# Adding two shifted exp readings by an accumulating DMA before PV, in an attention and MLP kernel

## Chip, cores and metric

One core of one Trainium2 chip. The metric is the device time of one launch in microseconds, the median of several runs of the same program. The engines are TensorE (PE in the profile; PEld is its loading of weights), VectorE (DVE), ScalarE (ACT), GpSimd (POOL) and SyncE (SP, which issues most DMAs here).

## The reference

Layer norm of x, then two branches that are added to x: attention with 32 query heads of 20 columns that share one head of keys and values, and an MLP with SiLU. S is 2048, D is 640, F is 1728.

```python
xn = _layernorm(x, axis=-1)
return x + _A_ref(xn, A_wq, A_wk, A_wv, A_wo) + _B_ref(xn, B_w1, B_w2)

# _A_ref, Dh = 20, H = 32
q = (x @ wq).reshape(B, S, H, Dh).transpose(0, 2, 1, 3)
k = x @ wk
v = x @ wv
scores = jnp.einsum("bhqd,bkd->bhqk", q, k) * (Dh ** -0.5)
p = _softmax(scores, axis=-1)
o = jnp.einsum("bhqk,bkd->bhqd", p, v)
o.transpose(0, 2, 1, 3).reshape(B, S, H * Dh) @ wo

# _B_ref
h = _silu(jnp.einsum("bsd,df->bsf", x, w1))
out = jnp.einsum("bsf,fd->bsd", h, w2)
```

## The kernel before

The scores are worked on in blocks of 128 keys by 512 queries of one head. 32 heads, 4 chunks of 512 queries and 16 blocks of keys make 2048 blocks. Four heads of one chunk form a group (64 blocks), and there are 32 groups. Heads sit in four slots of 32 rows or columns, so that TensorE runs up to four small matmuls side by side.

One step, `do_S`, takes three or four blocks. TensorE multiplies keys with queries (S, L1127) into one PSUM bank for each block. There are eight banks of 512 columns, one of which gathers the group's output. Then the blocks of the step are shared out:

- Most go to ScalarE: exp (L1161) over one, two or three banks at once, into a ring of `NBLK` blocks of results, E.
- Up to two go to VectorE: one instruction (L1176) scales and shifts the score so that its 16-bit integer, read as bf16, is a rough exp. Results go to Z, three blocks to a set (`ZB`). When a set is full, `flush_z` has GpSimd add a constant to Z twice (L1202, an integer add over four 16-bit numbers at a time), into Y0 and Y1. These are two more readings of the same rough exp, shifted by a part of an octave. The mean over the three readings, each with its weight, is close to the exp.

The weights are not multiplied onto the readings. V stands in memory three times, each copy scaled by the weight of its reading (`PH`), with a column for the sum of the softmax.

PV (`do_pv`, L968) multiplies these readings with V and adds into the group's bank: one matmul of 32 by 512 for a block from ScalarE, three for a block from VectorE (one each for Z, Y0, Y1). One to four of these, in different slots, run side by side as one set. When a group is done, its bank is copied out (L1245), transposed by a DMA, divided by the sum (L1231, L1236) and kept for the output projection.

Everything else of TensorE (query projections and MLP's first layer at L870 with 512 columns, MLP's second layer and output projection at L870 with 320) is cut into jobs that fill the room between S and PV.

The order of each engine's instructions is fixed when the program is built. A planner (`Sched`, with `step` as TensorE's choice) plays the program through with costs and latencies, and writes out each engine's list as it comes. The rules that choose between S, PV and jobs have some thirty numbers, and `SEG` holds a row of them for each 32 blocks. At run time each engine works its list in order, and waits on semaphores where an operand comes from elsewhere.

At the end no S is left: the last group's PV, the copy (L1245), its transposes on TensorE (L1252), reciprocal and multiply (L1231, L1236), transposes again (L1368), their copy (L1373), and the output projections of the last chunk (L870, 320 columns) follow, with the last evacuations (L1421 on ScalarE, L1424 on VectorE) and stores (L1428).

Of the kernel before, what the change touches and what calls it, by code (L numbers as in the profile page):

```python
# [8 lines left out]
BF16 = mybir.dt.bfloat16  # L9
# [7 lines left out]
P = 128  # L17
# [28 lines left out]
PH = ((0, 1.0), (43, 0.8046875), (86, 0.625))  # L46
ZMAX = 32512.0
# [3 lines left out]
NBLK = 35  # L51
NZ = 8
NY = 4
# [66 lines left out]
            "ACT4", "SPLIT", "U2", "LOOK", "W4", "M3")  # L120
SEG = (
# [366 lines left out]
class Builder:  # L488
# [20 lines left out]
    def alloc(self):  # L509
# [6 lines left out]
        self.qd = sb([P, 2, QW], BF16)  # L516
        self.wo = sb([P, DC, D], BF16)
        self.kT = sb([P, S], BF16)
        self.v = sb([P, 3, KT, SLOT], BF16)
        self.qT = sb([P, QS, QW], BF16)  # L520
        self.E = sb([P, NBLK * QW], BF16)
        self.Z = sb([P, NZ, ZB * QW], U16)
# [55 lines left out]
    def steps_init(self):  # L578
# [12 lines left out]
        self.pe_mode = None  # L591
        self.blk_pos = 0
        self.zset = 0
        self.yset = 0
        self.zblocks = []
        self.exp_op = {}
        self.dve_steps = 0
# [1285 lines left out]
```

## Time and profile before

| | |
|---|---|
| median of 3 runs | 669.32 us (669.15 to 669.32) |
| the profiled execution | 669.12 us, its span 667.3 us |
| granted TensorE clock | 1.00 |
| exp blocks on ScalarE, on VectorE | 1316, 732 |
| matmuls of PV (L968) | 3512 |
| instructions in all | 22800 |

The span runs from the first to the last instruction. The groups of the profile give busy time and the mean duration of one instruction. Durations contain the way through the engine's pipeline, so that consecutive instructions overlap, and the distance between two starts is shorter than a duration. For matmuls the ends are modelled. Idle time of an engine is put down to what ended it.

### The profile page before, as it was taken

How to read it: one execution, taken by the hardware profiler on the slowest of the kernel's cores; microseconds unless marked ns; L12 is line 12 of the kernel's file. 1: busy time of each engine (PE TensorE's matmuls, PEld its weight loads, DVE VectorE, ACT ScalarE, POOL GpSimd, SP SyncE). 2: the span in 40 equal slices, each digit the busy share in tenths (PEclk: the TensorE clock that was granted, in tenths of full speed). 3: DMA queues.
4: the chain of work that ended last, by engine and by line, in shares of the span. 5: the costliest groups of instructions: out<-in, count | busy, mean ns of one | idle time of the engine just before them, and what ended most of it. 6: DMA issues, size and time to landing. Idle time of an engine off the chain costs nothing.

```text
span 667.3 us, 22800 instructions
## 1 busy us (share of the span) xinstructions
PE 659.4 (99%) x9735; PEld 220.4 (33%) x9735; DVE 601.3 (90%) x1085; ACT 647.7 (97%) x737; POOL 404.6 (61%) x509
## 2 busy tenths in 40 slices
PE   8999999999999999999999999999999999999998
PEld 4432233332323322233333323233233333223345
DVE  7888999999989999999889999988999999998783
ACT  7999999999999999999999999999999999999993
POOL 2056457777486656676556653866767674676550
PEclk9999999999999999999999999999999999999999
DMA  7565201010012210000003110000002121001001
GB/s 211 110 213 150 73 14 12 2 26 2 18 44 62 57 10 17 3 10 18 19 10 84 41 32 17 10 10 18 10 13 47 38 57 37 10 10 31 5 11 41
DMA packets 51433, 26.73 MB, mean 40 GB/s; under 512 B 38566, under 2 KB 50694, under 8 KB 51334
## 3 DMA queue, kind: packets, MB, share of 16 engines
q1 hardware_dynamic: 51190, 25.12, 14.5%
q8 instruction: 78, 1.28, 0.8%
q14 instruction: 21, 0.17, 0.1%
q10 hardware_dynamic: 144, 0.16, 0.1%
HBM read 11.44 MB, written 2.62 MB: 21 GB/s over the span
## 4 chain that ended last, share of the span: by engine, by line
PE 87%; ACT 7%; DVE 3%; SPq 1%; DMA 1%; issue 0%; ACTq 0%
PE psall L968 33%; PE psall L1127 28%; PE psall L870 26%; ACT sbt L1161 6%; DVE sbt L1176 2%; ACT sbt L1336 1%; SPq L1531 1%; DMA sbt<-in_A_x_dram 1%; DVE sbt L1424 0%; PE psall L1326 0%; DVE sbt L1236 0%; ACT sbt L1620 0%; DVE sbt L1666 0%; DVE sbt L1771 0%; ACT sbt L1655 0%
## 5 line engine op out<-in xcount | busy, mean ns | idle before, releaser
L1161 ACT ACTIVATE sbt<-psall 128x1024 bf16<-128x1024 f32 (+2 forms) x649 | 620.1, 1129 | 3.5 <-PE psall L1127 2.6
L1202 POOL INT64_ADD sbt<-sbt x492 | 399.7, 827 | 244.4 <-DVE sbt L1176 171.3
L1176 DVE TENSOR_SCALAR sbt<-psall 128x512 uint16<-128x512 f32 x732 | 473.1, 683 | 46.3 <-PE psall L1127 37.1
L968 PE MATMUL psall<-sbt 128*32 128x512 bf16 x3512 | 265.0, 383 | 0.2
L1127 PE MATMUL psall<-sbt 32*128 32x512 bf16 x2048 | 245.8, 384 | 2.1 <-ACT sbt L1161 0.7
L870 PE MATMUL psall<-sbt 128*32 128x320 bf16 (+2 forms) x3923 | 220.7, 331 | 0.5 <-DVE sbt L1176 0.4
L1127 PEld LDWEIGHTS psall<-sbt 32*128 32x128 bf16 x2048 | 61.9, 91 | 241.4 <-ACT sbt L1161 161.1
L870 PEld LDWEIGHTS psall<-sbt 128*32 128x32 bf16 x3923 | 84.6, 95 | 84.6 <-issue 54.4
L968 PEld LDWEIGHTS psall<-sbt 128*32 128x32 bf16 x3512 | 64.4, 95 | 101.3 <-issue 64.6
L1336 ACT ACTIVATE sbt<-psall 128x512 bf16<-128x512 f32 x54 | 39.6, 739 | 0.0
L1341 DVE SCALAR_TENSOR_TENSOR sbt<-sbt,psall 128x512 bf16<-128x512 bf16 x54 | 36.6, 682 | 2.6 <-ACT sbt L1336 1.2
L1245 DVE CAST sbt<-psall 128x512 bf16<-128x512 f32 x32 | 21.8, 681 | 5.4 <-PE psall L968 5.3
L1236 DVE TENSOR_TENSOR sbt<-sbt 128x320 bf16<-128x320 bf16 x31 | 18.3, 591 | 0.1
L846 PE MATMUL psall<-sbt 128*128 128x512 bf16 (+4 forms) x55 | 15.2, 428 | 1.2 <-DVE sbt L1590 1.2
L1424 DVE SCALAR_TENSOR_TENSOR sbt<-psall,sbt 128x320 bf16<-128x320 f32 x28 | 13.1, 477 | 2.9 <-PE psall L870 2.9
L1405 DVE SCALAR_TENSOR_TENSOR sbt<-psall,sbt 128x320 bf16<-128x320 f32 x28 | 13.5, 483 | 1.6 <-PE psall L870 1.4
L1294 DVE TENSOR_SCALAR sbt<-psall 128x512 bf16<-128x512 f32 (+1 forms) x19 | 12.9, 680 | 0.1
L1635 DVE BATCH_NORM_STATS2 sbt<-sbt 128x6 f32<-128x320 bf16 x22 | 10.0, 470 | 0.9 <-DMA sbt<-in_A_x_dram 0.7
L1421 ACT ACTIVATE sbt<-psall 128x320 bf16<-128x320 f32 x4 | 1.7, 438 | 8.7 <-PE psall L870 8.7
L846 PEld LDWEIGHTS psall<-sbt 128*128 128x128 bf16 x55 | 5.5, 109 | 9.1 <-issue 4.0
L1231 DVE RECIPROCAL sbt<-sbt 128x16 f32<-128x16 bf16 x31 | 7.5, 243 | 0.0
L1620 ACT ACTIVATE sbt<-sbt 128x640 bf16<-128x640 bf16 x5 | 3.6, 730 | 3.2 <-DMA sbt<-in_A_x_dram 3.2
(57 smaller groups left out, 70.1 us busy)
## 6 DMA issues: line engine op xcount, KB each, us to landing
sbt<-in_A_x_dram SPq DMA_DIRECT2D x32, 160.0 KB, 3.2
out_dram<-sbt SPq DMA_DIRECT2D x15, 160.0 KB, 2.0
sbt<-in_B_w_dram SPq DMA_DIRECT2D x5, 432.0 KB, 5.3
sbt<-sbt SPq DMA_DIRECT2D x105, 20.0 KB
sbt<-in_B_w_dram SPq DMA_DIRECT2D x13, 160.0 KB, 3.1
sbt<-sbt SPq DMA_TRANSPOSE x58, 2.5
sbt<-in_A_wo_dram SPq DMA_DIRECT2D x5, 160.0 KB, 3.1
sbt<-in_A_wq_dram SPq DMA_DIRECT2D x5, 140.0 KB, 3.1
```

The lines of the kernel that those rows point to most:

```text
L846: return pe.matmul(self.bk(b, 0, n), self.zero[:, 0:P], self.zero[:, 0:n], start=True, stop=True)
L870: ins = pe.matmul(self.bk(b, 0, n, r, r + SLOT), w[:, r:r + SLOT], x, start=start, stop=stop, tile_position=(0, r), skip_group_check=True)
L968: ins = pe.matmul(self.bk(ub[k], 0, QW, r, r + SLOT), self.v[:, it.w, it.kt, :], it.x(), start=f, stop=False, tile_position=(0, r), skip_g ...
L1127: ins = pe.matmul(self.bk(bank[x]), self.kT[r:r + SLOT, kt * P:(kt + 1) * P], self.qT[r:r + SLOT, g % QS, :], start=True, stop=True, tile_ ...
L1161: return a.activation(self.E[:, b0 * QW:(b0 + na) * QW].rearrange("p (b n) -> p b n", n=QW), src, AF.Exp, scale=ACT_SCALE)
L1176: return v.tensor_scalar(self.Z[:, zs, zp * QW:(zp + 1) * QW], self.bk(bb), OFF, ZMAX, ALU.add, ALU.min)
L1202: sc.new("pool", YP_FIX + YP_BLK * n, lambda g, k=k: g.int64_add(self.Y[:, ys, k, 0:w].bitcast(I64), self.Z[:, zs, 0:w].bitcast(I64), PH[k ...
L1236: sc.new("dve", t_dve_ps(16 * DH), lambda v: v.tensor_tensor(dst, ut[:, :, :, 0:DH], rb, ALU.mult), [key, ("rL", up)], [("o", h0 + i) for ...
L1245: sc.new("dve", t_dve_ps(QW), lambda v: v.tensor_copy(self.U[:, up, :], self.bk(ub)), [("B", ub)], [("U", up)], prio=U_PRIO, name=f"Uev{g}")
L1336: sc.new("act", t_act(QW), lambda a: a.activation(t, src, AF.Tanh, scale=0.5), [("B", b)], [("tb", tp)], prio=TH_PRIO, name=f"th{c}_{fk}") ...
L1341: sc.new("dve", t_dve_ps(QW), lambda v: v.scalar_tensor_tensor(out=self.hT[0:rows, fk, :], in0=t, scalar=1.0, in1=src, op0=ALU.add, op1=AL ...
L1405: sc.new("dve", t_dve_ps(320), lambda v: v.scalar_tensor_tensor(out=in1, in0=ps, scalar=0.5, in1=in1, op0=ALU.mult, op1=ALU.add), [("B", b ...
```

## The change

In `flush_z` a set of three blocks may now be merged: GpSimd makes both shifted readings as before, with other shifts (`PAIR`, 39 and 82), and then starts a DMA that adds Y1 onto Y0 in bf16 (L1221). PV then reads Y0 alone, with a fourth copy of V that has the weight `PAIR_W`. Such a block needs two PV matmuls. A set is merged if it holds three blocks, if the planner has GpSimd less than `MG` us behind TensorE, and if the group has at least `MG_END` blocks to go. The DMA adds 128 rows of 1536 bf16 numbers, 384 KB.

The planner counts the DMA with 1.1 us of GpSimd's time and a landing 4.0 us later. `MG` becomes a column of `SEG`, all rows of `SEG` have other numbers, and the ring of exp results has 34 blocks and no longer 35. The loops that fill V's copies run over four.

```diff
 PH = ((0, 1.0), (43, 0.8046875), (86, 0.625))
+PAIR = (39, 82)
+PAIR_W = 0.71875
+VW = tuple(w for _, w in PH) + (PAIR_W,)
+ACC_ISSUE = 1.1
+ACC_LAND = 4.0
+MG = 3.0
+MG_END = 16
 ZMAX = 32512.0
...
-NBLK = 35
+NBLK = 34
...
-            "ACT4", "SPLIT", "U2", "LOOK", "W4", "M3")
+            "ACT4", "SPLIT", "U2", "LOOK", "W4", "M3", "MG")
 SEG = (
-    (6.04, 3.723, 0.711, 0.248, 4, 4, 5, 1.38, 0.05, 0, 2.56, 6, 2.29, 0.4, 10, 6, 6, 54, 15, 31, 2, 0, 0, 1, 99, 0, 0, 1),
...
+    (6.375, 0.382, 0.113, 0.226, 4, 5, 8, 0.66, 0.05, 4.33, 2.053, 34, 2.57, 1.281, 10, 6, 10, 54, 26, 33, 0, 0, 0, 2, 99, 0, 0, 1, 2),
...
-        self.v = sb([P, 3, KT, SLOT], BF16)
+        self.v = sb([P, 4, KT, SLOT], BF16)
...
+        self.merged = 0
+        self.acc_no = [0] * NY
+        self.acc_sem = [self.sc.sem(f"acc{i}") for i in range(NY)]
...
+        g1 = self.zblocks[-1][1]
+        back = max(sc.t["pool"] - sc.t["pe"], 0.0) + sum(o.dur for o in sc.pend["pool"])
+        merge = n == ZB and back < MG and self.bp < GB * (g1 + 1) - MG_END
         for k in range(2):
-            sc.new("pool", YP_FIX + YP_BLK * n, lambda g, k=k: g.int64_add(
+            sh = PAIR[k] if merge else PH[k + 1][0]
+            sc.new("pool", YP_FIX + YP_BLK * n, lambda g, k=k, sh=sh: g.int64_add(
                 self.Y[:, ys, k, 0:w].bitcast(I64), self.Z[:, zs, 0:w].bitcast(I64),
-                PH[k + 1][0] * 0x0001000100010001), zk + [("lib",)], [("Y", ys, k, i) for i in range(n)],
+                sh * 0x0001000100010001), zk + [("lib",)], [("Y", ys, k, i) for i in range(n)],
                 prio=4.0, name=f"yp{k}")
+        if merge:
+            op = sc.dma("pool", lambda g: g.dma_start(
+                self.Y[:, ys, 0, 0:w].bitcast(BF16), self.Y[:, ys, 1, 0:w].bitcast(BF16), accum_op=ALU.add),
+                [("Y", ys, 1, i) for i in range(n)], [("Y", ys, 0, i) for i in range(n)], P * w * 2,
+                sem=self.acc_sem[ys], prio=3.9, name="acc")
+            op.dur = ACC_ISSUE
+            op.late = ACC_LAND - 2.0
+            self.acc_no[ys] += 1
+            op.inc_no = self.acc_no[ys]
+            self.merged += 1
         for i, (t, g, kt, j) in enumerate(self.zblocks):
-            for k in range(2):
-                self.item(g, j, kt, k + 1, lambda k=k, i=i: self.Y[:, ys, k, i * QW:(i + 1) * QW].bitcast(BF16),
-                          [("Y", ys, k, i)])
+            for k in range(1 if merge else 2):
+                self.item(g, j, kt, 3 if merge else k + 1,
+                          lambda k=k, i=i: self.Y[:, ys, k, i * QW:(i + 1) * QW].bitcast(BF16), [("Y", ys, k, i)])
             self.g_late[g] -= 1
...
-        for k in range(3):
-            pool(0.15, lambda g, k=k: g.memset(self.v[:, k, :, DH:DH + 1], 0.5 * PH[k][1]), [("v0",)],
+        for k in range(4):
+            pool(0.15, lambda g, k=k: g.memset(self.v[:, k, :, DH:DH + 1], 0.5 * VW[k]), [("v0",)],
...
-                for k in range(3):
+                for k in range(4):
                     sc.new("dve", 0.07 + m * DH / 960.0, lambda v, k=k: v.tensor_scalar(
-                        self.v[:, k, n0:n1, 0:DH], sv, PH[k][1], None, ALU.mult),
+                        self.v[:, k, n0:n1, 0:DH], sv, VW[k], None, ALU.mult),
```

The lines of the changed kernel have other numbers: S is L1137, PV L978, the jobs L880, the adds on GpSimd L1216, the DMA L1221, exp L1171, VectorE's blocks L1186. What moves shows in the lists of instructions, of which three places follow. A row is a line, an operation, destination and source, the shape, and a count of equal instructions in sequence.

GpSimd, some way into the first groups of the changed kernel. The names in brackets are the semaphores waited for: done_ and an engine's name, or acc0 to acc3 for the DMAs on the four sets of Y.

```order
L1216 ISA sbt<-sbt 128x768
L1221 DMA sbt<-sbt 128x1536 [waits done_pool]
L1216 ISA sbt<-sbt 128x768 [waits done_dve]
L1216 ISA sbt<-sbt 128x768
L1221 DMA sbt<-sbt 128x1536 [waits done_pool]
L1216 ISA sbt<-sbt 128x768 [waits acc0,done_dve]
L1216 ISA sbt<-sbt 128x768 [waits acc1,done_dve]
L1216 ISA sbt<-sbt 128x768 [waits done_pe] x2
```

Before, this list held adds alone (492). Now 125 DMAs stand between 496 adds, and adds that write a set of Y again wait for that set's DMA.

TensorE, a place in the first groups where a merged reading is used, in the changed kernel:

```order
L1137 MATMUL psall<-sbt 128x512 x2
L978 MATMUL psall<-sbt 32x512 [waits acc0]
L978 MATMUL psall<-sbt 32x512 x3
L978 MATMUL psall<-sbt 32x512 [waits done_pool]
L978 MATMUL psall<-sbt 32x512 x3
L1137 MATMUL psall<-sbt 128x512 [waits done_dve,done_act]
```

Before, PV waited for GpSimd's adds, never for a DMA. Now 125 reads wait for acc, and PV has 3137 matmuls in place of 3512.

TensorE behind the last S, before:

```order
L968 MATMUL psall<-sbt 32x512 x18
L870 MATMUL psall<-sbt 32x320 x8
L968 MATMUL psall<-sbt 32x512 x2
L870 MATMUL psall<-sbt 32x320 x20
L968 MATMUL psall<-sbt 32x512 x2
L870 MATMUL psall<-sbt 32x320 x28
L1252 MATMUL psall<-sbt 128x128 x4
L870 MATMUL psall<-sbt 32x320 x56
L1368 MATMUL psall<-sbt 128x128 x4
L870 MATMUL psall<-sbt 32x320 x176
```

and in the changed kernel, where L1276 and L1392 are the two kinds of transposes:

```order
L978 MATMUL psall<-sbt 32x512 x16
L880 MATMUL psall<-sbt 32x320 x28
L978 MATMUL psall<-sbt 32x512 x3
L880 MATMUL psall<-sbt 32x320 x12
L1276 MATMUL psall<-sbt 128x128 x4
L880 MATMUL psall<-sbt 32x320 x20
L1392 MATMUL psall<-sbt 128x128 x4
L880 MATMUL psall<-sbt 32x320 x68
```

288 matmuls of 320 columns stood behind the last S, and 128 stand there now.

126 rows, old and new, of the table SEG are left out of this document.

## The prediction, written before the changed kernel ran

> **What bounds the kernel now.** I read four views in this order: the busy times, the groups by form, the timeline of one ordinary stretch, and the timeline of the end. First the busy times and the chain of waits by engine.
>
> ```profile
> PE 659.4 (99%) x9735; PEld 220.4 (33%) x9735; DVE 601.3 (90%) x1085; ACT 647.7 (97%) x737; POOL 404.6 (61%) x509
> PE 87%; ACT 7%; DVE 3%; SPq 1%; DMA 1%; issue 0%; ACTq 0%
> ```
>
> TensorE and ScalarE both look full and the chain runs over TensorE. Busy time alone cannot tell which has room, since matmuls overlap. The groups by form (columns: shapes and count, then busy us and mean ns of one, then idle before) give the counts:
>
> ```profile
> L1161 ACT ACTIVATE sbt<-psall 128x1024 bf16<-128x1024 f32 x565 | 543.3, 1112 | 2.4 <-PE psall L1127 1.4 <-PE psall L968 0.3
> L1176 DVE TENSOR_SCALAR sbt<-psall 128x512 uint16<-128x512 f32 x732 | 473.1, 683 | 46.3 <-PE psall L1127 37.1
> L1202 POOL INT64_ADD sbt<-sbt x492 | 399.7, 827 | 244.4 <-DVE sbt L1176 171.3 <-PE psall L968 69.5 <-PE psall L1127 1.6
> L968 PE MATMUL psall<-sbt 128*32 128x512 bf16 x3512 | 265.0, 383 | 0.2
> L1127 PE MATMUL psall<-sbt 32*128 32x512 bf16 x2048 | 245.8, 384 | 2.1 <-ACT sbt L1161 0.7 <-DVE sbt L1786 0.4 <-DVE sbt L1637 0.3
> L1161 ACT ACTIVATE sbt<-psall 128x1536 bf16<-128x1536 f32 x51 | 76.3, 1526 | 1.1 <-PE psall L1127 1.1
> L1336 ACT ACTIVATE sbt<-psall 128x512 bf16<-128x512 f32 x54 | 39.6, 739 | 0.0
> L1161 ACT ACTIVATE sbt<-psall 128x512 bf16<-128x512 f32 x33 | 20.2, 810 | 0.0
> ```
>
> What an instruction really occupies is the distance between starts. The timeline of one stretch (start, duration, engine and line, count) shows it:
>
> ```profile
> 18.07 0.60 PE L1127 MATMUL psall<-sbt 32*128 32x512 bf16 x5 [0.41 <-DVE sbt L1786]
> ...
> 251.65 0.74 ACT L1336 ACTIVATE sbt<-psall 128x512 bf16<-128x512 f32 x1
> 252.13 1.18 ACT L1161 ACTIVATE sbt<-psall 128x1024 bf16<-128x1024 f32 x1
> 253.03 0.76 ACT L1336 ACTIVATE sbt<-psall 128x512 bf16<-128x512 f32 x1
> ...
> 256.60 0.39 PE L1127 MATMUL psall<-sbt 32*128 32x512 bf16 x3
> 256.92 0.83 PE L968 MATMUL psall<-sbt 128*32 128x512 bf16 x12
> 257.68 0.10 PEld L1127 LDWEIGHTS psall<-sbt 32*128 32x128 bf16 x4 [0.42 <-ACT sbt L1161]
> 257.69 0.39 PE L1127 MATMUL psall<-sbt 32*128 32x512 bf16 x4
> 257.83 1.63 POOL L1202 INT64_ADD sbt<-sbt  x2 [0.39 <-DVE sbt L1176]
> 258.01 0.12 PEld L968 LDWEIGHTS psall<-sbt 128*32 128x32 bf16 x8 [0.23 <-issue]
> 258.13 4.50 DVE L1176 TENSOR_SCALAR sbt<-psall 128x512 uint16<-128x512 f32 x7 [0.40 <-PE psall L1127]
> ```
>
> Matmuls of four tiles run side by side as one set. Twelve L968 matmuls are three sets: 0.83 - 0.39 = 0.44 us for two, so a set is about 0.216. From S (scores, L1127) at 256.60 to the next kind at 256.92 is 0.32, so a change of kind costs 0.105 beside the set; PV at 256.92 to S at 257.69 is 0.77 = 3 x 0.216 + 0.12, the same again. On ScalarE a tanh of 512 takes 0.48 (251.65 to 252.13) and an exp of 1024 takes 0.90 (252.13 to 253.03). The end of the program:
>
> ```profile
> 648.43 5.65 ACT L1161 ACTIVATE sbt<-psall 128x1024 bf16<-128x1024 f32 x6
> 651.54 0.39 PE L1127 MATMUL psall<-sbt 32*128 32x512 bf16 x2
> 654.57 0.69 DVE L1245 CAST sbt<-psall 128x512 bf16<-128x512 f32 x1 [5.26 <-PE psall L968]
> 655.41 0.40 PE L1252 MATMUL psall<-sbt 128*128 128x128 bf16 x4
> 655.93 0.25 DVE L1231 RECIPROCAL sbt<-psall 128x16 f32<-128x16 f32 x1
> 656.21 0.49 DVE L1236 TENSOR_TENSOR sbt<-psall,sbt 128x320 bf16<-128x320 f32 x1
> 657.75 0.40 PE L1368 MATMUL psall<-sbt 128*128 128x128 bf16 x4
> 658.08 6.16 PE L870 MATMUL psall<-sbt 128*32 128x320 bf16 x176
> 658.28 0.41 DVE L1373 COPY sbt<-psall 128x512 bf16<-128x512 bf16 x1
> ```
>
> The 176 matmuls are 44 sets of (6.16 - 0.30) / 43 = 0.136.
>
> So the phase of exps has two limits. TensorE: first S at 18.07, last at 651.54, 633.5 us. The order of instructions has, between them, 882 PV sets, 627 S sets, 360 sets of 512 columns at L870, 540 of 320 columns, 1254 changes of kind and about 9 us of the rest: 190.5 + 135.4 + 77.8 + 73.4 + 131.7 + 9 = 618. Some 15 us are free. ScalarE: from 18.5 to 648.43 + 5.65 = 654.1, 635.6 us. Its work is 565 x 0.90 + 51 x 1.31 (1526 - 1112 = 414 ns more than the 1024 form) + 87 x 0.48 = 508.5 + 66.8 + 41.8 = 617. Some 18 us are free. Neither engine has 3% to spare. What one gives up, the other allows only up to its own 18. Behind the phase lies an end of 13.2 us (654.1 to 667.3) that TensorE sets.
>
> **The change part by part. PV.** In 125 of the three-block groups the two shifted readings become one, so PV reads two inputs a block and no longer three: 125 x 3 = 375 fewer L968 matmuls (3512 to 3137), 94 sets if all were full. The order holds fewer full ones. Between first and last S it has 804 PV sets, not 882 (78 x 0.216 = 16.8 us less), 636 S sets (+9, 1.9 us), 580 sets of 320 (+40, 5.4 us, output work drawn forward out of the end), one set of 512 less (0.2) and 1275 changes of kind (+21, 2.2 us). Fill matmuls are left out, as they stand where TensorE would wait. Together: -16.8 + 1.9 + 5.4 - 0.2 + 2.2 = **-7.5 us**.
>
> **ScalarE.** The 1316 exp blocks stay, in 602 of 1024, 27 of 1536 and 31 of 512: 37 x 0.90 - 24 x 1.31 - 2 x 0.48 = +0.9 us. Its free 18 us shrink to about 18 - 7.5 - 0.9 = 9.6, so it allows the -7.5. With both engines closer to full I give back 1 us for waits on each other (bounds 0 and 7.5: no row shows it; nearest is ScalarE's idle in front of L1161, 2.4 us for 565).
>
> **The end.** The two orders of TensorE behind the last S stand in the section on the change. 160 output matmuls moved ahead. Behind the second transposes stand 108 fewer, 27 sets x 0.136 = 3.7 us. Between the transposes stand 5 sets (0.7 us) in place of 14. There the chain cast, transpose, reciprocal, multiply now decides: the multiply ends at 656.21 + 0.49 = 656.7, so the second transposes start near 656.85 and not at 657.75: 0.9 us. Together **-4.6 us**; what remains (68 matmuls, 2.3 us) still covers the copy of 0.41.
>
> **The accumulating DMA.** Its price decides whether the saving arrives. On GpSimd's queue it stands right behind the two adds (L1216) that make its operands, and later adds wait for it by name (acc0, acc1), since they reuse its buffers; the rows stand in the section on the change. On TensorE the reading now waits for the DMA (acc0) where it waited for GpSimd alone, with the next S queued behind it, and ScalarE and VectorE waiting for that S.
>
> How much time does the order leave? For each merge I counted TensorE's work from the S that feeds the third block to the read that waits. A middle one has 10 S, 18 PV and 8 output sets and 19 changes: 28 x 0.216 + 8 x 0.136 + 19 x 0.105 = 9.1 us. Over all 125 the median is 9.3, a tenth lie under 7.7, the least is 6.8. Stretched by the 2.5% that TensorE idles: 9.5, 7.9, 7.0. Of this the way to the DMA takes 0.44 (S at 257.69, VectorE at 258.13) + 0.68 (L1176) + 1.63 (two adds) + about 0.2 for two semaphores = 2.95. Left from issue to landing: 6.5 us in the median, 4.9 for the tightest tenth, 4.0 at the least. The nearest rows of DMAs and issues:
>
> ```profile
> sbt<-sbt SPq DMA_DIRECT2D x1, 512.0 KB, 3.7
> out_dram<-sbt SPq DMA_DIRECT2D x15, 160.0 KB, 2.0
> L1428 SPq DMA_DIRECT2D out_dram<-sbt x15: 332/427/578, 204.9 to 664.8; - x15
> L1216 SPq DMA_TRANSPOSE sbt<-sbt x31: 1189/1209/1976, 55.3 to 636.2; - x31
> q1 hardware_dynamic: 51190, 25.12, 14.5%
> ```
>
> From 160 to 512 KB the landing grows by 1.7 us, 4.8 ns a KB. A plain copy of 384 KB would land in 2.0 + 224 x 0.0048 = 3.1 us; if the sum has to move twice the bytes, in 2.0 + 608 x 0.0048 = 4.9. Software on GpSimd may add to either; no row shows it. I take 4.5, nearer the upper end because the destination must be read as well. That lies under 6.5 and under 4.9: no stall, **0 us**. If that cover goes, each us of lateness costs TensorE up to 1 us at each of 125 reads.
>
> The Trainium skill, DMA: Bandwidth & Descriptors, section Anatomy of one DMA, puts a GpSimd DMA at 2.0 us plus bytes over 436 GB/s, which by estimate is 2.9 us here. For 512 KB it would say 3.2 where the row has 3.7, so the row decides; by either the sum is unchanged.
>
> GpSimd's issue is bounded by 0.43 (plain) and 1.21 (transpose): 125 of them take 54 to 151 us. I take 1.0, 125 us. GpSimd idles 667.3 - 404.6 = 262.7 us, so there is room; above 2.1 us each there is none. VectorE gets four more small copies of V and GpSimd a wider memset of V, both before 60 us and off both limits: 0. SyncE's DMAs share the 16 DMA engines: 125 x 0.39 MB = 49 MB come on top of 25 MB that took 14.5% of them, so they stay below half full, and the transposes of the output (L1216) have whole groups (some 20 us) to land: 0. The ring of exp results loses one of 35 blocks; ScalarE waited on its reader (L968) for 0.3 us in the row above, so 0.
>
> **Sum**, against the profiled execution of 669.1 us (span 667.3): 669.1 - 7.5 + 1.0 - 4.6 = **658.0**. The median of the runs is 669.3, 0.2 above; both round to the same forecast.
>
> **The rivals.**
>
> ScalarE does not give up its idle time. Its waits for S could be ones of latency (S needs the exp to free a bank, the exp needs S), which fewer PV sets do not shorten. For it: the weight loads of S wait 0.42 us for the exp at 257.68. Against it: right behind, TensorE is packed. Then only the end is won, and 0.9 lost: 669.1 - 4.6 + 0.9 = 665.4.
>
> ScalarE runs dense. With TensorE free by 16.8 us before the drawn-forward work, ScalarE's idle could fall to 5: 669.1 - 13 - 4.6 = 651.5. Against it: TensorE's remaining need allows only 7.5 unless its own 15 free us shrink too.
>
> The reads stall (slower). Place: the wait on acc at L978. If issue to landing takes 6.5 us, half of the 125 reads are late, by about 0.8 us each: some 50 us. At 7.5 nearly all are late by 1 on average: 125. The win of 11 is eaten where the mean stall over 125 is 0.09 us, at a landing near 5.2. For it: 4.9 is already my upper bound and software issue is not in it. Against it: half the reads leave 6.5. I price it at a landing of 6, some 30 us of stall: 658 + 30 = 688. The Trainium skill, DMA: Bandwidth & Descriptors, section Rules for kernel authors, says that an accumulating DMA reads its destination and writes it later, which speaks for this rival; no row before the change shows such a DMA.
>
> That the merge does little is no rival of weight: 375 matmuls are gone from the order.
>
> **How the numbers follow.** Forecast 0.57, between 653 and 664. Idle stays, 665: 0.12. Dense, 651: 0.10. Stall, above 671: 0.16. Small losses of the new order that eat the win: 0.05. The range 650 to 669 leaves out the stall and the rim of the dense case. A measurement here tells about 0.2% (1.3 us) from no change: faster 0.79, same 0.05, slower 0.16.
>
> **What would show it.** L978 with 3137 matmuls and about 237 us busy (265.0 x 3137 / 3512); 13.2 us behind the last exp become about 8.6; the exp phase becomes 629 long, with ScalarE idle in it near 10. In the list of waits, TensorE behind the DMA should stand below 3 us, GpSimd's issues should fit its gaps, the DMA should land in 4 to 5 us. I am wrong if TensorE waits for L1221 for more than 10 us, or if ScalarE's idle stays at 18.

## The result, and the profile after

| | before | after |
|---|---|---|
| median (lowest to highest, 4 runs each) | 669.32 us (669.15 to 669.33) | 692.12 us (690.47 to 692.85) |
| the profiled execution, its span | 669.1, 667.3 us | 690.5, 688.7 us |
| granted TensorE clock | 1.00 | 0.988 |
| first exp to the end of the last | 18.5 to 654.1: 635.6 us | 18.7 to 680.2: 661.5 us |
| ScalarE in it, from distances of starts, up to the start of its last: work, idle | 619.2, 15.3 us | 619.4, 40.6 us |
| behind the last exp | 13.2 us | 8.5 us |

The change is slower: 1.034 times the time before, with a 95% interval of 1.032 to 1.036. The end became 4.7 us shorter, and the phase of the exps 26 us longer. ScalarE's work stayed the same; what grew is its idle time, by 25 us.

First the busy times, the chain of waits by engine, some groups, the DMA queue of GpSimd and its landing, from the page of the changed kernel. A group's row ends with busy us, mean ns of one, and the idle time before it.

```profile
PE 656.0 (95%) x9372; PEld 217.4 (32%) x9372; DVE 609.4 (88%) x1089; ACT 651.3 (95%) x748; POOL 516.7 (75%) x639
q0 software_dynamic: 18000, 49.16, 38.3%
PE 64%; DVE 16%; DMA 11%; POOL 4%; ACT 3%; issue 2%; SPq 0%; POOLq 0%
L1216 POOL INT64_ADD sbt<-sbt x496 | 428.4, 959 | 129.7 <-DVE sbt L1186 104.2
L978 PE MATMUL psall<-sbt 128*32 128x512 bf16 x3137 | 252.4, 387 | 10.3 <-DMA sbt<-sbt 7.9
L1221 POOL DMA_DIRECT2D sbt<-sbt x125 | 112.4, 899 | 31.2 <-POOL sbt L1216 28.1
L1260 DVE TENSOR_TENSOR sbt<-sbt 128x320 bf16<-128x320 bf16 x31 | 26.3, 849 | 0.1
sbt<-sbt POOLq DMA_DIRECT2D x125, 384.0 KB, 4.2
```

Before, the chain was 87% TensorE, 3% VectorE and 1% DMA. Now DMA is 11% of it and VectorE 16%. The accumulating DMA itself is as forecast: 0.90 us to issue, 4.2 us to land in the median. Yet TensorE is busy for 95% of the span, no longer 99%. The list of waits of the changed kernel (who waits, for what: us in all, times, longest) names the places:

```profile
ACT sbt L1171 <- PE psall L1137: 25.3, 25, 6.4
PEld psall L978 <- DMA sbt<-sbt: 11.3, 11, 5.8
PE psall L978 <- DMA sbt<-sbt: 7.9, 6, 5.3
PE psall L880 <- DMA sbt<-sbt: 2.8, 2, 2.4
PE psall L1137 <- DVE sbt L1186: 2.8, 4, 1.2
DVE sbt L1255 <- DMA sbt<-sbt: 2.7, 4, 1.0
PE psall L880 <- issue: 2.4, 1, 2.4
```

ScalarE waits for S, 25.3 us in 25 places, 6.4 at one. TensorE's own waits are few and long. 5.3 of the 7.9 us at L978 are one wait (its weight load shows the same one with 5.8), and two at L880 are of 2.4 us. That is no late landing at all 125 readings. It is three kinds of places, and four single readings beside them that come 0.3 to 1.1 us early (at 400, 495, 558 and 624 us).

**The first accumulating DMA.** Two pieces of the chain of waits around it (start, us, what), and then the timeline of the same stretch:

```profile
33.19 1.64 POOL sbt L1216 x2
35.13 10.18 DMA sbt<-sbt
```

```profile
45.35 0.62 PE L978 MATMUL psall<-sbt 128*32 128x512 bf16 x4 [5.29 <-DMA sbt<-sbt]
46.56 1.02 ACT L1171 ACTIVATE sbt<-psall 128x1024 bf16<-128x1024 f32 x1 [6.41 <-PE psall L1137]
47.42 0.61 PE L1137 MATMUL psall<-sbt 32*128 32x512 bf16 x3
47.96 0.62 PE L880 MATMUL psall<-sbt 128*32 128x512 bf16 x4
52.98 0.39 PE L1137 MATMUL psall<-sbt 32*128 32x512 bf16 x3
53.30 0.61 PE L978 MATMUL psall<-sbt 128*32 128x512 bf16 x8
```

It lands after 10.18 us, beside weights whose loads SyncE issued from 32.6 to 35.7 us (the 16 DMA engines are busy for 98% of 33 to 40 us), and TensorE stands still for 5.29. Behind that, TensorE is slow: from S to the next kind it is 47.96 - 47.42 = 0.54 us, where it is 53.30 - 52.98 = 0.32 a little later. Only from about 52 on is it fast again.

**Two sets of output transposes.** SyncE transposes the attention output by DMA (L1379) for the output projection (L880, 320 columns). The timeline of the second place:

```profile
367.04 8.76 SPq L1379 DMA_TRANSPOSE sbt<-sbt  x4
368.80 0.88 POOL L1221 DMA_DIRECT2D sbt<-sbt  x1 [0.30 <-POOL sbt L1216]
372.87 1.53 PE L880 MATMUL psall<-sbt 128*32 128x320 bf16 x20 [2.43 <-DMA sbt<-sbt]
374.98 1.02 ACT L1171 ACTIVATE sbt<-psall 128x1024 bf16<-128x1024 f32 x1 [2.67 <-PE psall L1137]
```

TensorE waits 2.43 us for the transposes, and ScalarE behind it 2.67. The first place, at 206 us, looks alike, though the list puts its 2.39 us on "issue" and not on a DMA; the run without the DMAs around the transposes, below, settles it. The transposes' time from issue to landing, from the view of their line, before the change:

```profile
DMA to landing us min/median/max: 2.4/2.5/4.0
```

and after it:

```profile
DMA to landing us min/median/max: 2.4/5.1/7.2
```

The windows of the changed kernel (length, busy time of the engines, granted clock, share of the DMA engines, GB/s) show the three places, a quiet stretch, and one that is busier still:

```profile
40.00:60.00 20.00, 14.71 (x157) 3.42 (x157) 10.49 (x19) 11.70 (x14) 9.03 (x12) 0.74 0.67 143
60.00:80.00 20.00, 19.18 (x263) 5.64 (x255) 17.42 (x28) 19.72 (x26) 13.28 (x18) 1.00 0.91 240
200.00:220.00 20.00, 17.61 (x239) 5.49 (x236) 15.43 (x27) 16.03 (x19) 13.10 (x16) 0.91 0.68 120
280.00:300.00 20.00, 20.00 (x306) 6.41 (x302) 18.99 (x34) 20.00 (x23) 18.14 (x23) 1.00 0.38 68
360.00:380.00 20.00, 17.57 (x250) 5.99 (x247) 15.91 (x28) 16.69 (x21) 11.67 (x14) 0.91 0.77 123
```

In each of the three, the DMA engines are busy for two thirds or more (before: 29%, 20% and 18% in the same stretches), and the clock falls behind the gap. Busy DMA engines alone make no gap: from 60 to 80 us they are busy for 91%, with the clock at 1.00. A reader must stand close behind the late transfer.

**VectorE's multiply.** It divides a group's output by the softmax sum (L1260, both operands in SBUF). Its row before the change, where it is L1236:

```profile
L1236 DVE TENSOR_TENSOR sbt<-sbt 128x320 bf16<-128x320 bf16 x31 | 18.3, 591 | 0.1
```

The timeline of one place in the changed kernel:

```profile
438.71 2.07 DVE L1260 TENSOR_TENSOR sbt<-sbt 128x320 bf16<-128x320 bf16 x1
439.01 1.21 POOL L1221 DMA_DIRECT2D sbt<-sbt  x1
439.62 1.83 POOL L1216 INT64_ADD sbt<-sbt  x1
440.71 0.68 DVE L1186 TENSOR_SCALAR sbt<-psall 128x512 uint16<-128x512 f32 x1
441.53 0.39 PE L1137 MATMUL psall<-sbt 32*128 32x512 bf16 x3 [1.19 <-DVE sbt L1186]
```

The multiply takes 2.07 us where its mean was 0.59 before. Here it overlaps with GpSimd's issue, which takes 1.21 and not 0.88, and the add behind that takes 1.83 and not 0.8. VectorE's next block comes late, and TensorE waits 1.19 us for it. Over 1.2 us take 7 of the 32 multiplies; the longest before took 1.07.

But this place is the exception among the seven. In the other six at most 0.06 us of the multiply lie within an issue; beside them lie adds. The longest of the seven, and then a multiply that lies within an issue:

```profile
666.42 0.92 POOL L1221 DMA_DIRECT2D sbt<-sbt  x1
667.03 2.78 POOL L1216 INT64_ADD sbt<-sbt  x3
667.38 2.79 DVE L1260 TENSOR_TENSOR sbt<-sbt 128x320 bf16<-128x320 bf16 x1
670.82 0.40 PE L978 MATMUL psall<-sbt 128*32 128x512 bf16 x4 [2.02 <-DVE sbt L1186]
```

```profile
474.52 0.87 POOL L1221 DMA_DIRECT2D sbt<-sbt  x1
474.88 0.48 DVE L1260 TENSOR_TENSOR sbt<-sbt 128x320 bf16<-128x320 bf16 x1
```

Each of the six ends 0.35 us behind the end of an add (here 667.03 + 2.78 = 669.81, and 667.38 + 2.79 = 670.17), as the long ones before the change did. Five multiplies that lie within an issue for 0.41 us or more took 0.48 or 0.49. So it is the adds that the multiply waits for, and the issue changes the adds: 88 of the 124 adds that stand next behind an issue start before it ends, mostly by 0.27 us, and they and the add behind them are recorded with about 1.15 us and not 0.83 (186 of 496 adds take over 1.05 us, 8 of 492 before). They start 0.80 us apart as before, and so overlap by 0.35 us and not by 0.03. That this overlap is what keeps the multiply out is not shown: in the run with a plain copy, below, one multiply took 2.42 us beside three adds that overlap by 0.03.

In sum, TensorE's gaps of more than 0.25 us grew from 3.3 us to 26.4 over the span. The low clock behind them costs up to 0.012 x 688.7 = 8.3 us on top. What this did to ScalarE can be added up from the distances of its starts. Its delays of more than 0.4 us are 26.4 us in sum: 8.9 at the first DMA and in the slow stretch behind it, 9.1 behind output transposes (the two sets, and 0.9 at 539 us), 5.9 behind long multiplies and 2.4 behind three of the single readings. In the run without any DMA, below, they are 1.3.

### The profile page after: what moved, and what is told of

The parts are those of the page before. It is cut to its first block, busy times and chain, and to the rows that moved or that the text cites. A ratio compares the mean times of both kernels' runs of the same rounds, so it can differ in the third digit from the quotient of the medians.

```text
span 688.7 us, 22283 instructions
## 1 busy us (share of the span) xinstructions
PE 656.0 (95%) x9372; PEld 217.4 (32%) x9372; DVE 609.4 (88%) x1089; ACT 651.3 (95%) x748; POOL 516.7 (75%) x639
## 3 DMA queue, kind: packets, MB, share of 16 engines
q0 software_dynamic: 18000, 49.16, 38.3%
## 4 chain that ended last, share of the span: by engine, by line
PE 64%; DVE 16%; DMA 11%; POOL 4%; ACT 3%; issue 2%; SPq 0%; POOLq 0%
PE psall L978 24%; PE psall L1137 21%; PE psall L880 18%; DMA sbt<-sbt 10%; DVE sbt L1186 9%; POOL sbt L1216 4%; ACT sbt L1171 3%; DVE sbt L1260 2%; DVE sbt L1365 1%; DVE sbt L1659 1%; POOL sbt L1221 1%; DVE sbt L1269 1%; DMA sbt<-in_A_x_dram 1%; DVE sbt L1255 0%; PE psall L847 0%
## 5 line engine op out<-in xcount | busy, mean ns | idle before, releaser
L1171 ACT ACTIVATE sbt<-psall 128x1024 bf16<-128x1024 f32 (+2 forms) x660 | 620.9, 1073 | 26.1 <-PE psall L1137 25.3
L1216 POOL INT64_ADD sbt<-sbt x496 | 428.4, 959 | 129.7 <-DVE sbt L1186 104.2
L1186 DVE TENSOR_SCALAR sbt<-psall 128x512 uint16<-128x512 f32 x732 | 474.0, 682 | 54.0 <-PE psall L1137 46.3
L978 PE MATMUL psall<-sbt 128*32 128x512 bf16 x3137 | 252.4, 387 | 10.3 <-DMA sbt<-sbt 7.9
L1137 PE MATMUL psall<-sbt 32*128 32x512 bf16 x2048 | 250.9, 386 | 8.7 <-DVE sbt L1186 2.8
L880 PE MATMUL psall<-sbt 128*32 128x320 bf16 (+2 forms) x3923 | 228.6, 334 | 6.4 <-DMA sbt<-sbt 2.8
L1137 PEld LDWEIGHTS psall<-sbt 32*128 32x128 bf16 x2048 | 62.9, 91 | 246.9 <-ACT sbt L1171 163.5
L1221 POOL DMA_DIRECT2D sbt<-sbt x125 | 112.4, 899 | 31.2 <-POOL sbt L1216 28.1
L880 PEld LDWEIGHTS psall<-sbt 128*32 128x32 bf16 x3923 | 84.9, 96 | 93.3 <-issue 59.2
L978 PEld LDWEIGHTS psall<-sbt 128*32 128x32 bf16 x3137 | 60.6, 95 | 109.8 <-issue 71.3
L1360 ACT ACTIVATE sbt<-psall 128x512 bf16<-128x512 f32 x54 | 37.1, 687 | 0.3 <-PE psall L880 0.3
L1260 DVE TENSOR_TENSOR sbt<-sbt 128x320 bf16<-128x320 bf16 x31 | 26.3, 849 | 0.1
L856 PE MATMUL psall<-sbt 128*128 128x512 bf16 (+3 forms) x44 | 11.1, 408 | 1.2 <-DVE sbt L1614 1.2
L1255 DVE RECIPROCAL sbt<-sbt 128x16 f32<-128x16 bf16 x31 | 7.6, 244 | 2.7 <-DMA sbt<-sbt 2.7
```

The lines of the kernel that those rows point to most:

```text
L880: ins = pe.matmul(self.bk(b, 0, n, r, r + SLOT), w[:, r:r + SLOT], x, start=start, stop=stop, tile_position=(0, r), skip_group_check=True)
L978: ins = pe.matmul(self.bk(ub[k], 0, QW, r, r + SLOT), self.v[:, it.w, it.kt, :], it.x(), start=f, stop=False, tile_position=(0, r), skip_g ...
L1137: ins = pe.matmul(self.bk(bank[x]), self.kT[r:r + SLOT, kt * P:(kt + 1) * P], self.qT[r:r + SLOT, g % QS, :], start=True, stop=True, tile_ ...
L1171: return a.activation(self.E[:, b0 * QW:(b0 + na) * QW].rearrange("p (b n) -> p b n", n=QW), src, AF.Exp, scale=ACT_SCALE)
L1186: return v.tensor_scalar(self.Z[:, zs, zp * QW:(zp + 1) * QW], self.bk(bb), OFF, ZMAX, ALU.add, ALU.min)
L1216: sc.new("pool", YP_FIX + YP_BLK * n, lambda g, k=k, sh=sh: g.int64_add(self.Y[:, ys, k, 0:w].bitcast(I64), self.Z[:, zs, 0:w].bitcast(I64 ...
```

## The experiments

Three explanations were tried. The *transfer*: the bytes being added make landings late, the readings' or the transposes'. The *issue*: issuing the DMA on GpSimd costs time there and on VectorE. The *order*: the new sequence loses time by itself. Letters in the expectations stand for the first (A), the second (B) and the third (C). All ratios are to the kernel before, run beside them (669.4 to 669.5 us).

**A thin DMA.** It adds 32 of the 1536 columns; the rest of Y1 is left out of the sum. All else is unchanged.

```diff
-                self.Y[:, ys, 0, 0:w].bitcast(BF16), self.Y[:, ys, 1, 0:w].bitcast(BF16), accum_op=ALU.add),
+                self.Y[:, ys, 0, 0:32].bitcast(BF16), self.Y[:, ys, 1, 0:32].bitcast(BF16), accum_op=ALU.add),
```

> The changed kernel with the same order on every engine, where each of the 125 accumulating DMAs adds 32 of the 1536 columns (8 KB, not 384); the rest of the merged sum is left out, so the output is not the reference's. Theory A (the loss comes from the bytes: first merges and output transposes land late beside 49 MB of new traffic, TensorE stands, and its clock drops behind each stand): 657 to 664 us, TensorE's gaps above 0.25 us under 5 us in sum (25 in the changed kernel), no window with a clock under 0.97. Theory B (the loss comes from GpSimd's issue and what it blocks on VectorE): 685 to 692. Theory C (the planner's new order is itself slower): 685 to 692, without any DMA waits.

674.87 us (673.64 to 676.57), 1.0089 [1.0072, 1.0105]. Some rows of its page:

```profile
q0 software_dynamic: 18000, 1.03, 5.1%
L1216 POOL INT64_ADD sbt<-sbt x496 | 428.1, 966 | 114.1 <-DVE sbt L1186 95.2
L1260 DVE TENSOR_TENSOR sbt<-sbt 128x320 bf16<-128x320 bf16 x31 | 26.2, 846 | 0.1
sbt<-sbt POOLq DMA_DIRECT2D x125, 8.0 KB, 2.1
```

The time lies between what the transfer (657 to 664) and the issue (685 to 692) would have given: neither is the whole. The bytes are worth 692.1 - 674.9 = 17.2 us. The transposes land in 2.5 us again, and of the gaps before the output projections one of 0.7 us is left. The adds (966 ns) and the multiply (846 ns) are as long as in the changed kernel: that part belongs to the issue, not to the bytes.

**No DMA.** The same order on every engine, with a small memset of GpSimd in place of each DMA; Y1 is left out of the sum.

```diff
+        for op in self.order["pool"]:
+            if op.name == "acc":
+                op.dma, op.inc_no, op.fn = False, None, self.stand_in
...
+            sc.stand_in = lambda g: g.memset(self.flag[:, 0:1], 0.0)
```

> The same order, with a one-column memset on GpSimd in the place of each DMA: no DMA, no issue of 0.88 us; the addition is left out. Theory A: as with the thin DMA, within 2 us of it (657 to 664). Theory B: 657 to 664 here while the thin DMA stays near 690. Theory C: 685 to 692. The reciprocal's multiply on VectorE (849 ns in mean in the changed kernel, 591 before): under B near 600 here, under A unchanged with the thin DMA's.

664.55 us (663.87 to 665.67), 0.9928 [0.9913, 0.9942]. Its groups by form, where the add is L1219, PV L981, the multiply L1264:

```profile
L1219 POOL INT64_ADD sbt<-sbt x496 | 400.8, 819 | 228.7 <-DVE sbt L1189 201.9 <-PE psall L981 23.6 <-PE psall L1140 2.8
L981 PE MATMUL psall<-sbt 128*32 128x512 bf16 x3137 | 249.0, 384 | 0.2
L1264 DVE TENSOR_TENSOR sbt<-sbt 128x320 bf16<-128x320 bf16 x31 | 17.8, 573 | 0.1
```

Adds (819 ns) and multiply (573 ns) are as before the change, and TensorE no longer waits at PV. So the order itself does not lose. All of the loss, 692.1 - 664.6 = 27.5 us, is the DMA: 17.2 by its bytes, 10.3 by being issued and landing at all. What the order wins is 669.5 - 664.6 = 4.9 us, and nearly all of that is the end: in the profiled executions the phase of exps went from 635.6 to 634.9, the end from 13.2 to 8.5. ScalarE's idle time went from 15.3 to about 14 only, with 375 PV matmuls fewer.

**A plain copy.** The same bytes are copied and not added; Y0 is overwritten, so its sum holds only Y1.

```diff
-                self.Y[:, ys, 0, 0:w].bitcast(BF16), self.Y[:, ys, 1, 0:w].bitcast(BF16), accum_op=ALU.add),
+                self.Y[:, ys, 0, 0:w].bitcast(BF16), self.Y[:, ys, 1, 0:w].bitcast(BF16)),
```

> The same order and the same 384 KB, moved by a plain copy and not added, so the sum is left out. If adding makes the transfer slow (the destination is read as well), landing falls from 4.2 to about 3.1 us and the time by some 10 us, to 675 to 685. If a copy through GpSimd's queue costs the same, landing stays at 4.2 and the time at 688 to 693.

674.65 us (672.01 to 675.97), 1.0072 [1.0049, 1.0095]. From its groups and its page:

```profile
L1221 POOL DMA_DIRECT2D sbt<-sbt x125 | 69.3, 554 | 31.1 <-POOL sbt L1216 26.7 <-issue 2.9 <-PE psall L978 0.6
L1260 DVE TENSOR_TENSOR sbt<-sbt 128x320 bf16<-128x320 bf16 x31 | 21.4, 690 | 0.1
```

```profile
q0 software_dynamic: 10000, 49.16, 18.8%
sbt<-sbt POOLq DMA_DIRECT2D x125, 384.0 KB, 2.7
```

Adding doubles what the DMA costs the 16 engines (38.3% against 18.8% for the same 49.16 MB, 144 packets each against 80), and the issue takes 0.90 us and not 0.55. The copy saves 17.5 us, as much as the thin DMA and just beyond the 675 to 685 expected, by a mixture: its issue is shorter, the adds start only behind it (818 ns), and its landing lies in between.

**The change without merges.** Three PV matmuls a block again, with the new numbers of the planner and the ring of 34.

```diff
-        merge = n == ZB and back < MG and self.bp < GB * (g1 + 1) - MG_END
+        merge = False and n == ZB and back < MG and self.bp < GB * (g1 + 1) - MG_END
```

> The changed kernel's table, 34 blocks and fourth copy of V, but no set is merged: PV has 3512 matmuls again. If the table alone carries a loss: above 675. If the loss is the DMA's: 668 to 674, close to before, since the table was made for fewer matmuls.

681.91 us (681.77 to 684.5), 1.0194 [1.0176, 1.0213], with ScalarE idle for 31.0 us. By what was expected, a time above 675 would mean that the table alone carries a loss. But the new numbers were found for the merged program: without merges they lose 12 us, while in the merged order, without the DMA, they lost none. So runs in which the planner makes another order are no fair measure of a part; three of the next four groups show that again.

**Less PV in the kernel before.** Every ninth call of PV multiplies 32 columns and not 512 (378 matmuls, some 95 sets; a matmul's mean falls from 383 to 183 ns, so by estimate 19 us of TensorE); the rest of these columns is left out of the output. The order is that of before.

```diff
+        cut = self.npv % 9 == 0 and not any(first)
...
+                if cut:
+                    ins = pe.matmul(self.bk(ub[k], 0, SLOT, r, r + SLOT), self.v[:, it.w, it.kt, :], it.x()[:, 0:SLOT],
...
```

> The kernel before, same order, where every ninth PV set (95 of 889, 378 matmuls) runs over 32 columns and not 512; 480 columns of these products are left out. TensorE has 95 x 0.2 = 19 us less to do, nothing else changes. Theory of the prediction (TensorE's load sets the exp phase): 650 to 662 us. Rival (ScalarE sets it, its idle of 15 us is not given up): 666 to 670, with ScalarE's phase of exps still near 635 us.

666.9 us (666.66 to 667.12), 0.9962 [0.9947, 0.9977]: 19 us less for TensorE win 2.5. Together with the run without the DMA this says that, in these two orders, the phase of exps has no 7.5 us to give to a shorter PV.

**Merges only from block 224 of 2048 on.** Meant to take away the first, late DMA.

```diff
-        merge = n == ZB and back < MG and self.bp < GB * (g1 + 1) - MG_END
+        merge = self.bp >= 224 and n == ZB and back < MG and self.bp < GB * (g1 + 1) - MG_END
```

> The changed kernel, where no set is merged before block 224 (about 90 us), while the weights are loading: 101 merges. Theory A (the first merges stand behind the loads, TensorE stands 5.3 us and its clock is low for 6 us behind): 680 to 685 us, 7 to 11 less than the changed kernel, no window with a clock under 0.9 ahead of 90 us. If the early stall costs nothing later: 690 to 693.

707.11 us (705.3 to 708.77), 1.0562 [1.0543, 1.0582]. The stall at 40 us is gone (ScalarE idles 1.5 us between 20 and 80), but the planner made another order with 101 merges, and ScalarE idles 51 us over the whole. It says nothing on what the first DMA costs.

**The multiply on GpSimd.** Meant to take VectorE out of the way of the issue; only the last group's multiply stays.

```diff
-        sc.new("dve", t_dve_ps(16 * DH), lambda v: v.tensor_tensor(
+        sc.new("dve" if g == self.NG - 1 else "pool", t_dve_ps(16 * DH) if g == self.NG - 1 else 0.8, lambda v: v.tensor_tensor(
```

> The changed kernel, where the multiply of the normalisation (L1260, two operands in SBUF) runs on GpSimd and not on VectorE, all but the last group's; the planner, told 0.8 us, merges 98 sets. Theory B (VectorE's multiply stands while GpSimd issues an accumulating DMA, up to 2.8 us): the gaps of TensorE at those places (440, 456, 556, 575, 668 us, 6.5 us in sum) are gone, 680 to 686 us. If these gaps have another cause: 688 or more.

1095.72 us (1092.75 to 1098.71), 1.6359 [1.6317, 1.6401]. Two rows of its waits:

```profile
POOL sbt L1216 <- issue: 179.0, 30, 6.9
POOL sbt L1260 <- issue: 127.4, 18, 7.6
```

30 adds and 18 multiplies wait 6.0 and 7.1 us in the mean for nothing that the profile shows; adds alone have no such wait in the other runs. The trial says nothing on the multiply of VectorE.

**Output transposes counted 4 us later by the planner**, so that their readers come later.

```diff
+            op.late = 4.0 if not last else 0.0
```

> The changed kernel, where the planner counts the DMA transposes of the attention output (L1379) as landing 4 us later, so that the output projection stands later in TensorE's order; 125 merges. Theory A (transposes land at 5.1 in place of 2.5 us beside the accumulating DMAs, and TensorE stands 2.4 us at 206 and at 370): both gaps go, 682 to 687 us. If they land late only by what the planner already covers: 690 to 693.

696.9 us (696.8 to 702.27), 1.043 [1.0393, 1.0467]. The gaps at 206 and 370 us are gone; the other order costs more than they did (ScalarE idles 43.9 us), and a stall of 5.1 us that ends at 46 us stays. So it, too, prices nothing.

**Fixed order, some DMAs gone.** To price the three places without a new order, four runs keep the order of the changed kernel on every engine, and put the memset of the second run in place of the DMAs chosen; those readings leave Y1 out. The core, with the condition of the last run; the first three have one of its parts each:

```diff
+        oT = [o for o in self.order["sp"] if o.name == "oTd"]
+        nrm = [o for o in self.order["dve"] if o.name[:3] == "nrm"]
...
+            if op.name == "acc" and (op.start < 60.0 or any(o.start - 6.0 < op.start < o.end + 5.0 for o in oT) or any(op.start - 1.2 < o.start < op.start + 2.0 for o in nrm)):
+                op.dma, op.inc_no, op.fn = False, None, self.stand_in
```

The 6 DMAs of the first 60 us:

> The changed kernel's order on every engine; the 6 accumulating DMAs of the first 60 us are replaced by a one-column memset on GpSimd, and their additions left out, 119 stay. Theory A by parts: the stall of 5.3 us at 40 us and the low clock behind it go, 682 to 685 us (692 - 8). If the time behind is made up later anyway: 690 to 693.

The 14 around the output transposes:

> The same order; the 14 DMAs issued from 6 us ahead of a transpose of the attention output to 5 us behind it are replaced in the same way, 111 stay. If these DMAs hold up the transposes: the gaps of 2.5 us at 206 and 370 and the low clock behind them go, 683 to 686 us. If the transposes are late from the general load: 690 to 693.

The 26 whose issue is planned around a multiply:

> The same order; the 26 DMAs planned from 2.0 us ahead of a normalising multiply on VectorE (L1260) to 1.2 us behind it are replaced in the same way, 99 stay. Theory B: the multiply's mean falls from 849 to under 650 ns and the gaps at 440, 456, 556, 575, 668 go, 682 to 686 us. If the multiply stands for another reason: 690 or more, mean unchanged.

All 41 of these (some are in two sets), so that 84 stay:

> The same order; all three sets are replaced, 41 in all, and 84 DMAs stay. If the three causes are separate and make up the loss: 665 to 670, within 5 us of the kernel without any DMA (664.6). If the loss goes with the number of DMAs: 692 - 28 x 41 / 125 = 683.

| DMAs gone | median (lowest to highest) | ratio | against 692.1 |
|---|---|---|---|
| 6, early | 684.98 (682.92 to 691.18) | 1.0252 [1.0194, 1.031] | -7.1 |
| 14, transposes | 682.93 (681.04 to 691.0) | 1.0223 [1.0162, 1.0285] | -9.2 |
| 26, multiply | 680.86 (678.68 to 682.97) | 1.0169 [1.014, 1.0198] | -11.3 |
| 41, all three | 671.93 (668.74 to 679.4, 10 runs) | 1.0035 [1.001, 1.0061] | -20.2 |
| 125 (the run above) | 664.55 | 0.9928 | -27.5 |

Each set gives something back, 7 to 11 us, in intervals that are 4 to 8 us wide. Singly they give back 27.6 us in sum, together 20.2: some DMAs are in two sets, and how much of the rest is noise stays open. The places show what changed. Without the early DMAs the stall of 5.3 us is gone, and without those around the transposes both gaps of 2.4 us are. Without those around the multiplies the gaps at 456, 556 and 668 us are gone, but those at 440 and 575 stay (1.3 and 1.0 us), and a reading waits 3.1 us at 539 us, where none waits in the changed kernel. The multiply of this run, L1270, is back near its old time, though not under the 650 ns expected:

```profile
L1270 DVE TENSOR_TENSOR sbt<-sbt 128x320 bf16<-128x320 bf16 x31 | 20.7, 666 | 0.1
```

The profile of the last of the four was taken at the upper end of its spread, so only its time is used. If the loss went with the number of DMAs, it should have taken 683 us. It took 671.9: 41 of 125 DMAs cost 20 us, 0.5 each; the 84 others cost 671.9 - 664.6 = 7.4 us, 0.09 each.

No run gives a program that computes the whole sum and beats the kernel before. The new end is worth 4.7 us; whether the old PV leaves room to draw its work forward was not tried.

## Why the prediction was wrong

**The end, -4.6 us: right.** It went from 13.2 to 8.45 us (8.6 was forecast), and the run without DMAs wins 4.9 in all.

**The phase of exps, -7.5 us and +1.0 given back: wrong in its allowance.** TensorE's work shrank as counted, but "it allows the -7.5" does not hold: with the DMA out of the way, ScalarE's idle fell by about 1 us and the phase by 0.7. Cutting 19 us of PV from the old kernel won 2.5. ScalarE's free 18 us (15.3 by the distances of all its starts) are mostly not time that a shorter PV gives back. The first rival said so, priced 665.4, and 664.55 is what the order makes without the DMA; it had been given 0.12. That ScalarE's waits are ones of latency is the rival's reason; these runs show that the idle time stays, and not why.

**The accumulating DMA, 0 us: wrong, and the step that decided.** It cost 27.5 us. The prices put into it were right in the median: 4.5 us to land (4.2 measured), 1.0 to issue (0.90). What failed is to take one landing for all 125 (37 took more than the upper bound of 4.9), and to weigh it only against the readings of its own sum. Three sentences fell:

- "That lies under 6.5 and under 4.9: no stall". One DMA of the 125, the first, landed in 10.18 us beside the weight loads. It cost 5.3 us of stall and more by the low clock: 8.9 us of ScalarE's delays, and about 7 in time when the early DMAs are gone.
- The transposes "have whole groups (some 20 us) to land: 0", as the DMA engines "stay below half full". They did not even in the mean: the new queue took 38.3% where a plain copy of these bytes took 18.8%, on top of 16.0%. In the two stretches concerned they were 68 and 77% busy, the transposes in front of the output projection took 5.1 us and not 2.5, and two readers came 2.4 us early. About 9 us. The 20 us were those of the transposes of a group's output (L1216 before), whose reader, the reciprocal (L1255), waits for 2.7 us in all; the transposes in front of the output projection (L1355 before, L1379 now) and their readers were not named at all.
- "GpSimd idles 262.7 us, so there is room". There is: GpSimd's busy time grew by 112.1 us (404.6 to 516.7), about the 112.4 us of the issues. But the issue also changes the adds behind it, which overlap more, and the multiply of VectorE waits for one to three of them (573 ns in the mean without the DMA, 849 with it). About 6 us by ScalarE's delays, 11 by the run without the DMAs around the multiplies. The work queued behind the multiply, VectorE's blocks and so S, was not named at all.

The rival of stalling reads was near in time (688 against 692), but not for its reason. It let each landing be 6 us and half of the reads late. The landing was 4.2 in the median, and apart from the first DMA the readings waited little: the 7.9 us of PV's wait in the list hold the 5.3 of one place.

**The tests that were named.** PV has 3137 matmuls, as said; its busy time is 252 us and not 237, and still 249 without the DMA, as busy time of overlapping matmuls does not go with their number. TensorE's wait for the DMA is 7.9 us (11.3 by its weight loads): not under 3, and about the 10 that were to refute the forecast. ScalarE's idle "near 10" is 40.6. The line to watch would have been TensorE's waits for any DMA and for VectorE, not for L1221 alone.

## What to carry to other kernels

A DMA that is added to a tight schedule must be weighed at its worst place and not by its median: 41 of the 125 here cost 0.5 us each, the other 84 less than a tenth. For a new transfer ask three things of each stretch: what it shares the DMA engines with there, who reads those other transfers next, and what the issuing engine's next instructions hold up on its neighbours. And a saving on one engine is worth only what the engine behind it gives back: cut that work crudely in the old kernel first, and read what the time does.

## What was not expected of the hardware

**A gap costs TensorE its clock.** Behind 5.29 us of idling the granted clock was 0.50 for 6.4 us (45.35 to about 51.8) and 1.00 from 52 us on; behind 2.43 us it was 0.50 for some 3 (372.9 to 376.2, sets of 320 columns at 0.28 us in place of 0.136). The length of the gap alone does not decide: behind 2.02 us at 670.8 the clock stayed at 1.00, while in the run with the thin DMA it was 0.50 from 654 to 656, behind a gap of 2.01 us in the same place. The Trainium skill, TensorE: Matmul & The Clock Gate, section Part 1: The HAM clock gate, gives about 3.4 us of idling for the fall and as much of work for the rise. The long gap agrees with the fall; here shorter gaps sufficed, and behind the long one the rise took 6.4 us of work.

**A multiply on VectorE waits for the adds of GpSimd, also for adds that start later.** Of the 17 multiplies over 1.2 us in the changed kernel and the runs with the thin DMA, the copy and the DMAs around the multiplies gone, 15 end 0.35 or 0.36 us behind the end of an add. The longest (2.79 us) started at 667.38 and let adds from 667.83 and 668.63 go first. The Trainium skill, SBUF — State Buffer, section Who interferes with whom, says that a VectorE instruction with two inputs in SBUF contends with a GpSimd instruction that reads SBUF. The adds agree with that. Of the issue of a DMA the section says that a tensor_tensor was not seen to stall it; the five multiplies of 0.48 or 0.49 us within an issue agree in so far as neither was long there. The two of the 17 that lie on an issue of 1.2 us (439 us in the changed kernel, 423 with the thin DMA) remain open, and so does why an add that starts later goes first.

**Adding in the DMA costs twice a copy on the DMA engines**, and 0.90 us in place of 0.55 at the issue, by the rows of the copy run.

**Changing between two kinds of instruction on GpSimd took 6 to 7 us** at 30 adds and 18 multiplies, in the run with the multiply there. The Trainium skill, GPSIMD Engine Reference, section 2.1 Instruction dispatch, gives some 6 us for loading code at the first call of a fresh kernel; the rows agree with the size, though no row shows a load.
